# Attention's scores on four quarters of the array, and a unit's outputs in the burst of the next unit's state products

## The chip, the cores and the metric

The kernel runs on one core of a Trainium2 chip. The metric is device time in microseconds (us) of one execution; before the change the median of 3 runs is 1006.01 us (1004.19 to 1006.75).

## The reference, cut to what matters

The first part is a gated linear recurrence over 768 time steps for 4 batches and 8 heads of width 48; its output, as 3072 tokens of width 384, goes through two feed-forward layers.

```python
for t in range(S):
    state = f[:, :, t, :, None] * state + np.einsum('bhd,bhe->bhde', k[:, :, t], v[:, :, t])
    y[:, :, t] = np.einsum('bhd,bhde->bhe', q[:, :, t], state)
...
h = x @ w_in                      # 384 -> 2048, a piecewise square as activation, then 2048 -> 384
...
return (silu * val @ w_out)       # gate and value 384 -> 1536, product, then 1536 -> 384
```

## The kernel before, in words

**Feed-forward passes.** The 3072 tokens are cut into 6 groups of 512. The first layer and the second each take a group in one pass, so there are 12 passes, in the order of `PASSES` (line 34): two groups in layer 1, the same two in layer 2, and so on. A float32 product is made of three matmuls of 128x128 weights with 512 columns (`mm3`, lines 374 to 377: high by high, high by low, low by high), and nine of these (three pieces of 384) are a chunk of the planner: `lin` (578) writes `hp`, `gps` or `vps`, `o_mm` (616) adds to `acc`. During the first pass of each layer the weights, which arrive as 64-bit numbers, are turned into these halves by VectorE, ScalarE and GpSimd (`c_b` to `c_l`, 329 to 360); later passes load them again from DRAM.

**Attention units.** The recurrence is done in 24 units of 128 time steps of one batch (`NU`, line 22), four to a group of tokens. A unit holds its 8 heads as 4 pairs, and its time as two halves of 64 (`C`), so there are 8 blocks. Its steps are:

- `at_k`, `at_q` (460, 465): scaled keys and queries, with rows 0 to 47 for one head of a pair and rows 64 to 111 for the other;
- `at_pe1a` (476): the scores, 16 products of 64x64 over 48 rows. Rows 64 to 111 write partitions 0 to 63 of `psa`, rows 0 to 47 write partitions 64 to 127. All eight blocks lie in one PSUM bank. Each float32 product is two matmul instructions in the trace, so a unit has 32;
- `at_pe1t` (484): four transposes of the keys into `pst`, which ScalarE copies to `kn` (`at_kn`, 503);
- `at_msk` (493): VectorE multiplies the scores by the causal triangle, in two instructions of 64x512, into `ma` and `mb`;
- `at_pe2` (509): the state products of both time halves into `psu0` and `psu1`, 16 products that use rows 0 to 63 and 64 to 127, and both halves of the columns;
- `at_state` (519) on VectorE and `at_state_out` (530) on ScalarE: the new state after each half, copied into `vs`;
- `at_pe3` (535): the outputs `psy` from masked scores and state, 16 products over 112 or 128 rows; `at_yc` (546) copies them to `y`, and for every second unit `at_yd` (556) moves `y` by six DMAs into `xl`, the input of the layer-1 pass; `split_h` and `split_l` (379, 382) make the high and low half of it.

**What sets the order.** Nothing is scheduled at run time. `Planner` (line 49) takes operations with an engine, an estimated duration, dependencies, a priority and buffer slots to take and give. For each engine it takes the ready operation with the smallest priority and writes its instructions, so the engines' queues are fixed, in order, when the kernel is built. Lines 683 to 748 add the attention's operations with priorities around `at_base(u)` (677); the feed-forward's follow in lines 788 to 863. PSUM has eight banks: `at` 3, `h` 2, `acc0` to `acc2`. Before the change `psa`, `pst`, the two `psu` and `psy` all take slots of `at`: `pa` one, `pt` one, `p2` two, `p3` one. Ahead of the first pass TensorE is filled with dummy matmuls (`fill`, 642, tile `wt`).

Of the kernel before, what the change touches and what calls it, by code (L numbers as in the profile page):

```python
# [19 lines left out]
C = 64  # L20
# [28 lines left out]
class Planner:  # L49
# [6 lines left out]
    def add(self, eng, dur, fn, deps=(), prio=0.0, take=(), give=(), lat=None, order=()):  # L56

        lat = lat if lat is not None else {"PE": 0.3, "Pool": 0.25}.get(eng, 0.15)
        deps, order = (tuple(d for d in x if d is not None) for x in (deps, order))
        self.ops.append(dict(eng=eng, dur=dur, fn=fn, deps=deps, order=order, prio=prio, take=take, give=give, lat=lat))  # L60
        return len(self.ops) - 1
# [202 lines left out]
def fast_path(ctx: ExitStack, tc: tile.TileContext, qk, xx, vv, w1, w2, fi, out):  # L264
# [208 lines left out]
        a = A[u]  # L473
        nc.scalar.copy(a["mb"][0:64], a["ma"][0:64])

    def at_pe1a(u):
        a = A[u]
        psa = ps.tile([128, 8, C], F32, tag="at", name="psa", bufs=3)
        for i in range(8):
            nc.tensor.matmul(psa[0:64, i], a["k"][64:112, i], a["ma"][64:112, i], start=True, stop=True)  # L480
            nc.tensor.matmul(psa[64:128, i], a["k"][0:48, i], a["ma"][0:48, i], start=True, stop=True)
        a["psa"] = psa

    def at_pe1t(u):
        a = A[u]
        pst = ps.tile([128, NP, 112], F32, tag="at", name="pst", bufs=3)
        for p in range(NP):
            nc.tensor.transpose(
                pst[:, p], a["t"][:, COLS + p * TB:COLS + (p + 1) * TB], ident[0:112, 0:112]
            )  # L490
        a["pst"] = pst

    def at_msk(u):
        a = A[u]
        tb = tri.rearrange("p (o t) -> p o t", o=1)
        nc.vector.tensor_tensor(
            out=a["ma"][0:64], in0=a["psa"][0:64], in1=tb[0:64].to_broadcast([64, 8, C]), op=ALU.mult
        )
        nc.vector.tensor_tensor(
            out=a["mb"][64:128], in0=a["psa"][64:128], in1=tb[64:128].to_broadcast([64, 8, C]), op=ALU.mult  # L500
        )

    def at_kn(u):
        a = A[u]
        kn = ap_.tile([128, NP, 112], F32, tag="kn", name="kn", bufs=1)
        nc.scalar.copy(kn, a["pst"])
        a["kn"] = kn

    def at_pe2(u):
        a = A[u]  # L510
        a["psu"] = [ps.tile([112, NP, D], F32, tag="at", name=f"psu{c}", bufs=3) for c in range(2)]
        for p in range(NP):
            for c in range(2):
                r = slice(c * C, (c + 1) * C)
                psu = a["psu"][c]
                nc.tensor.matmul(psu[0:64, p], a["kn"][r, p, 0:64], a["vn"][r, 2 * p + 1], start=True, stop=True)
                nc.tensor.matmul(psu[64:112, p], a["kn"][r, p, 64:112], a["vn"][r, 2 * p], start=True, stop=True)
# [17 lines left out]
    def at_pe3(u):  # L535
        a = A[u]
        vs = VS[u % 2]
        psy = ps.tile([112, 8, C], F32, tag="at", name="psy", bufs=3)
        for p in range(NP):
            for c in range(2):  # L540
                i = 2 * p + c
                nc.tensor.matmul(psy[0:48, i], vs[0:112, 0, c, p], a["ma"][0:112, i], start=True, stop=True)
                nc.tensor.matmul(psy[64:112, i], vs[:, 1, c, p], a["mb"][:, i], start=True, stop=True)
        a["psy"] = psy
# [25 lines left out]
    def getX(n):  # L570
        if n not in X:
            X[n] = (xp.tile([128, KK, 512], F32R, tag="xh", name="xh"), xp.tile([128, KK, 512], F32R, tag="xl", name="xl"))
        return X[n]
# [103 lines left out]
    def at_base(u):  # L677
# [2 lines left out]
            return -40.0 + 7.0 * (u % 4)  # L680
        return begin[n - 1] + 4.0 + 15.0 * (u % 4)

    for u in range(NU):
        b = at_base(u)
        n = first1[u // 4]
        if u % 2 == 0:
            E["lx", u] = add("SP", 1.6, lambda u=u: at_loadx(u), (), b - 12, ("x",), (), 2.0, (E.get(("l", u - 1)),))
        E["l", u] = add("SP", 2.1, lambda u=u: at_load(u), (), b - 11.9, ("w" if u < 4 else "qk", "vn"), (), 2.0, (E["lx", u // 2 * 2], E.get(("l", u - 1))))
        E["lv", u] = add("SP", 1.1, lambda u=u: at_loadv(u), (E.get(("p3", u - 2)),), b - 4, (), (), 2.0, (E["l", u],))
        b0 = u // 2 * 2  # L690
        swap = u // 2 in (1, 3)
        if u == b0:
            F = {}

            def mk(u, i, F=F, swap=swap):
                F[i] = decay_ops(u, swap, i)
                F[i][0]()

            if u == 0:
                exs = [  # L700
                    add("ACT", 1.9 - 1.28 * i, lambda i=i, mk=mk: mk(0, i), (E["lx", 0],), b - 3 + i, () if i else ("e",)) for i in range(2)
                ]
                sgs = [add("ACT", 1.9 - 1.28 * i, lambda i=i, F=F: F[i][1](), exs, b - 3 + i) for i in range(2)]
                ads = [add("DVE", 0.45, lambda i=i, F=F: F[i][2](), (exs[i],), b - 2 + i) for i in range(2)]
                for i in range(2):
                    E["sg", i], E["ad", i] = sgs[i], ads[i]
            else:
                ex = add("ACT", 1.07 if u < 8 else 2.35, lambda u=u, mk=mk: mk(u, None), (E["lx", u],), b - 3, ("e",))
                sg = add("ACT", 2.35, lambda F=F: F[None][1](), (ex,), b - 3)
                if swap:  # L710
                    ex, sg = sg, ex
                ad = add("DVE", 0.75, lambda F=F: F[None][2](), (ex,), b - 2)
                for i in range(2):
                    E["sg", u + i], E["ad", u + i] = sg, ad
        odd = u != b0
        one, two = ("x", "e") if swap else ("e", "x")
        R = add("DVE", 1.5, lambda u=u: at_scan_r(u), (E["ad", u],), b)
        Pp = add("DVE", 1.28, lambda u=u: at_scan_p(u), (E["sg", u],), b + 0.2)
        pk = u in POOL_K
        k = add("Pool" if pk else "DVE", 1.8 if pk else 0.7, lambda u=u: at_k(u), (R, E["l", u], E.get(("k", u - 1))), b + 0.1, (), (one,) if odd else ())  # L720
        q = add("DVE", 0.72, lambda u=u: at_q(u), (Pp, E["l", u]), b + 0.4, ("ma", "mb"))
        E["k", u] = k
        so0 = None if u < B else add("ACT", 0.72, lambda u=u: at_state_out(u, 0), (E.get(("st", u - B)), E.get(("p3", u - 2))), b + 1)
        qc = add("ACT", 0.62, lambda u=u: at_qc(u), (q,), b + 1.5)
        pa = add("PE", 1.05, lambda u=u: at_pe1a(u), (k, q), b + 1, ("at",))
        pt = add("PE", 0.35, lambda u=u: at_pe1t(u), (pa,), b + 1.1, ("at",), ("w" if u < 4 else "qk",))
        kn = add("ACT", 0.55, lambda u=u: at_kn(u), (pt,), b + 2, ("kn",), ("at",))
        mask = add("DVE", 1.4, lambda u=u: at_msk(u), (pa, qc), b + 2.5, (), ("at",))
        p2 = add("PE", 0.8, lambda u=u: at_pe2(u), (kn, E["l", u]), b + 3, ("at", "at"), ("kn", "vn"))
        s0 = add("DVE", 0.37 if u < B else 0.75, lambda u=u: at_state(u, 0), (p2, so0, E.get(("st", u - B))), b + 2.2, (), ("at",))  # L730
        so1 = add("ACT", 0.72, lambda u=u: at_state_out(u, 1), (s0, E.get(("p3", u - 2))), b + 2.2)
        s1 = add("DVE", 0.75, lambda u=u: at_state(u, 1), (so1, E.get(("st", u - 1)) if odd else None), b + 4, (), ("at", two) if odd else ("at",))
        E["st", u] = s1
        p3 = add("PE", 1.1, lambda u=u: at_pe3(u), (mask, qc, so1, E["lv", u], E.get(("yc", u - 1))), b + 4, ("at",), ("ma", "mb"))
        E["p3", u] = p3
        E["yc", u] = add("ACT", 1.18, lambda u=u: at_yc(u), (p3,), b + 4, () if odd else ("y",), ("at",))
        if odd:

            tk = ("X",) if u % 4 == 1 else ()
            yd = add(  # L740
                "SP", 3.5, lambda u=u, n=n: at_yd(u, getX(n), u % 4 - 1), (E["yc", u], E["yc", u - 1]), b + 4, tk, ("y",), 2.2,
                (("tx", n),),
            )
            if tk:
                takeX[n] = yd
            sl = slice((u % 4 - 1) * TB, (u % 4 + 1) * TB)
            sh = add("ACT", 0.85, lambda n=n, sl=sl: split_h(*getX(n), sl), (yd,), b + 5)
            E.setdefault(("x", n), []).append(add("DVE", 1.05, lambda n=n, sl=sl: split_l(*getX(n), sl), (sh,), b + 5))
    E["fin"] = add("DVE", 0.6, finish, [E["st", u] for u in range(NU)], 1e6)


# [199 lines left out]
```

## Time and profile before

| | before |
|---|---|
| median of 3 runs | 1006.01 us |
| profiled execution | 1004.98 us |
| span of its trace | 1002.9 us |
| TensorE busy | 966.2 us, 6596 matmuls |
| VectorE busy | 577.5 us |
| ScalarE busy | 490.0 us |
| mean granted TensorE clock | 0.992 |

The span is the time from the first to the last instruction in the trace; the other 2.1 us of the profiled execution lie around it. A matmul's end is modelled in the trace, so two that follow each other overlap in it: the distance from start to start is what one costs. "Busy" adds up what is covered, whether or not it holds anything up.

### The profile page before, as it was taken

What the parts mean: (1) busy time and instruction counts of PE and PEld (TensorE: products, weight loads), DVE (VectorE), ACT (ScalarE), POOL (GpSimd) and SP (SyncE); (2) the same over time, 40 slices, a digit from 0 to 9 for tenths busy, and PEclk for the clock granted to TensorE, in tenths of its full rate; (3) what the DMA queues carried; (4) which work ended last, traced back from release to release, by engine and by line L of the source; (5) the groups of instructions that cost most, each with busy time, mean ns of one, the idle gap of its engine ahead of it and who ended that gap; (6) DMA issues with size and microseconds to landing.
All of it is one profiled execution on the core that took longest, in us unless ns stands there. A gap on an engine that the chain in (4) does not pass through costs nothing.

```text
span 1002.9 us, 16173 instructions
## 1 busy us (share of the span) xinstructions
PE 966.2 (96%) x6596; PEld 790.6 (79%) x6596; DVE 577.5 (58%) x792; ACT 490.0 (49%) x772; POOL 117.6 (12%) x78
## 2 busy tenths in 40 slices
PE   8978797999999999999999999999999999999997
PEld 8956575877878888788888888887877888888885
DVE  6899988986774566575633433474653333433332
ACT  6666576774543446576643212355564544212121
POOL 3344433442320000000000000000000000000000
PEclk9999898999999999999999999999999999999999
DMA  9677766657765676322755102677310554200001
GB/s 276 198 276 255 216 221 235 186 176 267 235 226 176 211 230 196 123 59 70 232 199 170 55 1 67 208 243 227 116 35 17 170 201 165 95 1 12 20 1 35
DMA packets 51954, 153.00 MB, mean 153 GB/s; under 512 B 5744, under 2 KB 25712, under 8 KB 51872
## 3 DMA queue, kind: packets, MB, share of 16 engines
q1 hardware_dynamic: 51872, 151.89, 47.0%
q8 instruction: 54, 0.88, 0.4%
q14 instruction: 28, 0.23, 0.1%
HBM read 110.97 MB, written 36.18 MB: 147 GB/s over the span
## 4 chain that ended last, share of the span: by engine, by line
PE 74%; DVE 10%; DMA 6%; issue 4%; ACT 3%; POOL 2%; SPq 0%; DVEq 0%; ACTq 0%; POOLq 0%
PE acc L375 9%; PE acc L376 9%; PE acc L377 9%; PE hp L375 5%; PE hp L376 5%; PE hp L377 5%; PE vps L375 4%; PE gps L375 4%; DMA raw<-w 4%; PE vps L376 4%; PE gps L376 4%; PE gps L377 4%; PE vps L377 4%; DVE raw L340 2%; PE psa L480 2%
## 5 line engine op out<-in xcount | busy, mean ns | idle before, releaser
L376 PE MATMUL acc<-gl,w 128*128 128x512 f32 x504 | 197.9, 393 | 2.5 <-POOL gl L613 1.8
L375 PE MATMUL acc<-gh,w 128*128 128x512 f32 x504 | 200.1, 397 | 0.0
L377 PE MATMUL acc<-gh,w 128*128 128x512 f32 x504 | 196.9, 391 | 0.0
L375 PE MATMUL hp<-xh,w 128*128 128x512 f32 x288 | 115.7, 402 | 11.4 <-DVE g L596 7.5
L604 DVE TENSOR_TENSOR sg<-gps,sg 128x512 f32<-128x512 f32 x72 | 49.7, 690 | 127.8 <-ACT sg L600 127.8
L376 PE MATMUL hp<-xl,w 128*128 128x512 f32 x288 | 113.4, 394 | 4.3 <-DVE xl L383 4.3
L376 PEld LDWEIGHTS acc<-gl,w 128*128 128x128 f32 x504 | 95.2, 189 | 23.6 <-POOL gl L613 3.3
L377 PE MATMUL hp<-xh,w 128*128 128x512 f32 x288 | 113.0, 392 | 0.0
L375 PEld LDWEIGHTS acc<-gh,w 128*128 128x128 f32 x504 | 95.2, 189 | 21.0 <-ACT gh L608 0.2
L596 DVE SCALAR_TENSOR_TENSOR g<-g,hp 128x512 f32<-128x512 f32 x96 | 65.6, 684 | 79.5 <-ACT g L593 79.3
L377 PEld LDWEIGHTS acc<-gh,w 128*128 128x128 f32 x504 | 95.2, 189 | 19.9
L600 ACT ACTIVATE sg<-gps 128x512 f32<-128x512 f32 x72 | 43.0, 598 | 133.3 <-PE gps L377 122.9
L589 ACT ACTIVATE g<-hp,half 128x512 f32<-128x512 f32 x96 | 66.0, 688 | 75.0 <-PE hp L377 70.5
L608 ACT CAST gh<-sg 128x512 fp32r<-128x512 f32 x72 | 44.7, 620 | 105.3 <-DVE sg L604 105.2
L375 PE MATMUL gps<-xh,w 128*128 128x512 f32 x216 | 85.1, 394 | 0.0
L356 POOL TENSOR_TENSOR w<-raw,w 128x768 fp32r<-128x768 f32 x34 | 70.3, 2066 | 124.6 <-ACT w L352 124.6
L375 PE MATMUL vps<-xh,w 128*128 128x512 f32 x216 | 84.7, 392 | 0.0
L377 PE MATMUL gps<-xh,w 128*128 128x512 f32 x216 | 84.1, 389 | 0.0
L376 PE MATMUL gps<-xl,w 128*128 128x512 f32 x216 | 84.1, 389 | 0.0
L376 PE MATMUL vps<-xl,w 128*128 128x512 f32 x216 | 84.1, 389 | 0.0
L377 PE MATMUL vps<-xh,w 128*128 128x512 f32 x216 | 84.1, 389 | 0.0
L608 ACT CAST gh<-g 128x512 fp32r<-128x512 f32 x96 | 59.5, 619 | 50.3 <-DVE g L596 46.0
(95 smaller groups left out, 1585.1 us busy)
## 6 DMA issues: line engine op xcount, KB each, us to landing
w<-w2d SPq DMA_DIRECT2D x36, 768.0 KB, 4.3
raw<-w SPq DMA_DIRECT2D x34, 768.0 KB, 6.6
w<-w1d SPq DMA_DIRECT2D x32, 768.0 KB, 4.9
w2d<-w SPq DMA_DIRECT2D x18, 768.0 KB, 8.2
w1d<-w SPq DMA_DIRECT2D x16, 768.0 KB, 7.3
qk<-qk SPq DMA_DIRECT2D x24, 448.0 KB, 5.5
x<-xx SPq DMA_DIRECT2D x11, 455.0 KB, 4.4
vn<-vv SPq DMA_DIRECT2D x24, 192.0 KB, 4.8
```

The costliest lines, as they stand in the source:

```text
L340: nc.vector.scalar_tensor_tensor(out=lo, in0=hi, scalar=3, in1=lo, op0=ALU.logical_shift_left, op1=ALU.bitwise_or)
L356: nc.gpsimd.tensor_tensor(out=w[:, :, 1, :], in0=jb["t"].rearrange("p (a n) -> p a n", a=2), in1=w[:, :, 0, :].bitcast(F32), op=ALU.subtract,)
L375: nc.tensor.matmul(o, w[:, 0, wsl], xh, start=first, stop=False)
L376: nc.tensor.matmul(o, w[:, 0, wsl], xl, start=False, stop=False)
L377: nc.tensor.matmul(o, w[:, 1, wsl], xh, start=False, stop=last)
L480: nc.tensor.matmul(psa[0:64, i], a["k"][64:112, i], a["ma"][64:112, i], start=True, stop=True)
L589: nc.scalar.activation(g, hp, AF.Relu, bias=half, scale=0.5)
L596: nc.vector.scalar_tensor_tensor(out=g, in0=g, scalar=1.0, in1=hp, op0=ALU.min, op1=ALU.max)
L600: nc.scalar.activation(sg, gps, AF.Sigmoid)
L604: nc.vector.tensor_tensor(out=sg, in0=p, in1=sg, op=ALU.mult)
L608: nc.scalar.copy(gh, g)
```

## The change

It has three parts.

- The scores of a unit go into two tiles, `psa0` and `psa1`, of four blocks each, in two PSUM banks. In `psa0` the rows and partitions are as before; in `psa1` rows 64 to 111 write partitions 64 to 127 and rows 0 to 47 write partitions 0 to 63. The products are written in an order that goes round these four. The mask is four VectorE instructions of 64x256.
- Scores and transposes are one operation of the planner (`at_pe1`). From unit 4 on it takes all three `at` slots at once; in the first four units its tiles lie in the banks of `acc1`, `acc2` and `h`, without slots of the planner.
- For u of 5 and more that is not the first of its group of four, the outputs of unit u-1 (`at_pe3`) are written right behind the state products of unit u (`at_pe2`) in one operation, which depends on what both need and takes three `at` slots. The last unit of each group, and units 0 to 3, keep an operation of their own for the outputs.

```diff
-    def at_pe1a(u):
...
-        psa = ps.tile([128, 8, C], F32, tag="at", name="psa", bufs=3)
-        for i in range(8):
-            nc.tensor.matmul(psa[0:64, i], a["k"][64:112, i], a["ma"][64:112, i], start=True, stop=True)
-            nc.tensor.matmul(psa[64:128, i], a["k"][0:48, i], a["ma"][0:48, i], start=True, stop=True)
+    def at_pe1(u):
+        tags, bufs = (("acc1", "acc2", "h"), (1, 1, 2)) if u < 4 else (("at",) * 3, (3, 3, 3))
...
+        psa = [ps.tile([128, 4, C], F32, tag=tags[e], name=f"psa{e}", bufs=bufs[e]) for e in range(2)]
+        for i in range(4):
+            for e in range(2):
+                n = i // 2 * 4 + e * 2 + i % 2
+                hi, lo = (slice(64, 128), slice(0, 64)) if e else (slice(0, 64), slice(64, 128))
+                nc.tensor.matmul(psa[e][hi, i], a["k"][64:112, n], a["ma"][64:112, n], start=True, stop=True)
+                nc.tensor.matmul(psa[e][lo, i], a["k"][0:48, n], a["ma"][0:48, n], start=True, stop=True)
...
+    def at_scores(u):
...
+            pv = a["psa"][e].rearrange("p (a c) t -> p a c t", c=2)
+            yield ma[0:64, :, e], pv[hi], hi
+            yield mb[64:128, :, e], pv[lo], lo
...
     def at_msk(u):
...
+        for to, of, r in at_scores(u):
+            nc.vector.tensor_tensor(out=to, in0=of, in1=tb[r].to_broadcast([64, 2, 2, C]), op=ALU.mult)
...
-        pa = add("PE", 1.05, lambda u=u: at_pe1a(u), (k, q), b + 1, ("at",))
-        pt = add("PE", 0.35, lambda u=u: at_pe1t(u), (pa,), b + 1.1, ("at",), ("w" if u < 4 else "qk",))
-        kn = add("ACT", 0.55, lambda u=u: at_kn(u), (pt,), b + 2, ("kn",), ("at",))
-        mask = add("DVE", 1.4, lambda u=u: at_msk(u), (pa, qc), b + 2.5, (), ("at",))
-        p2 = add("PE", 0.8, lambda u=u: at_pe2(u), (kn, E["l", u]), b + 3, ("at", "at"), ("kn", "vn"))
+        pa = pt = add("PE", 1.2, lambda u=u: at_pe1(u), (k, q), b + 1, ("at",) * 3 if u >= 4 else (), ("w" if u < 4 else "qk",))
+        kn = add("ACT", 0.55, lambda u=u: at_kn(u), (pt,), b + 2, ("kn",), ("at",) if u >= 4 else ())
+        mask = add("DVE", 1.7, lambda u=u: at_msk(u), (pa, qc), b + 2.5, (), ("at",) * 2 if u >= 4 else ())
+        fuse = u >= 5 and u % 4 > 0
+        pre = todo.pop() if fuse else None
+        p2 = add(
+            "PE", 1.9 if fuse else 0.8, lambda u=u, fuse=fuse: (at_pe2(u), at_pe3(u - 1) if fuse else None),
+            (kn, E["l", u]) + (pre["deps"] if fuse else ()), b + 3, ("at",) * (3 if fuse else 2),
+            ("kn", "vn") + (("ma", "mb") if fuse else ()),
+        )
+        if fuse:
+            leave(u - 1, p2)
...
-        p3 = add("PE", 1.1, lambda u=u: at_pe3(u), (mask, qc, so1, E["lv", u], E.get(("yc", u - 1))), b + 4, ("at",), ("ma", "mb"))
...
+        deps = (mask, qc, so1, E["lv", u])
+        if u < 4 or u % 4 == 3:
+            deps += (E.get(("yc", u - 1)),)
+            leave(u, add("PE", 1.1, lambda u=u: at_pe3(u), deps, b + 4, ("at",), ("ma", "mb")))
+        else:
+            todo.append(dict(deps=deps + (E.get(("yc", u - 1)),)))
```

`leave(u, p3)` holds, unchanged, what stood behind `p3` in the loop: the copy to `y`, the DMAs into `xl` and the two halves.

## Rows read from the trace of the kernel before

**Rows 1.** The page: span, busy time by engine, and the chain by engine.

```profile
span 1002.9 us, 16173 instructions
...
PE 966.2 (96%) x6596; PEld 790.6 (79%) x6596; DVE 577.5 (58%) x792; ACT 490.0 (49%) x772; POOL 117.6 (12%) x78
...
PE 74%; DVE 10%; DMA 6%; issue 4%; ACT 3%; POOL 2%; SPq 0%; DVEq 0%; ACTq 0%; POOLq 0%
```

**Rows 2.** Stretches: length, then busy us of PE, PEld, DVE, ACT, POOL; PEclk, DMA, GB/s.

```profile
0.00:52.00 52.00, 46.89 (x905) 44.42 (x905) 41.21 (x54) 34.22 (x51) 18.17 (x28) 1.00 0.81 239
52.00:151.00 99.00, 82.10 (x687) 64.10 (x687) 92.12 (x103) 65.55 (x106) 44.62 (x24) 0.97 0.72 242
151.00:300.00 149.00, 141.81 (x630) 114.81 (x631) 117.55 (x137) 88.84 (x125) 54.77 (x28) 0.98 0.68 219
300.00:780.00 480.00, 479.37 (x3424) 388.97 (x3424) 247.99 (x389) 233.64 (x385) 0.00 (x0) 1.00 0.43 138
...
151.00:161.00 10.00, 6.22 (x15) 4.64 (x16) 8.85 (x11) 5.91 (x8) 2.73 (x2) 0.67 0.86 302
```

**Rows 3.** Timeline of TensorE, scores of units 9 and 23: start, us, line, tile.

```profile
332.04 0.39 PE L377 MATMUL acc<-gh,w 128*128 128x512 f32 x1
332.36 0.27 PE L480 MATMUL psa<-ma,qk 48*64 48x64 f32 x1
332.37 0.27 PE L481 MATMUL psa<-ma,qk 48*64 48x64 f32 x1
...
333.29 0.22 PE L481 MATMUL psa<-ma,qk 48*64 48x64 f32 x1
333.44 0.60 PE L488 MATMUL pst<-ident,qk 112*128 112x112 f32 x4
...
334.12 0.39 PE L376 MATMUL gps<-xl,w 128*128 128x512 f32 x1
...
763.09 0.27 PE L480 MATMUL psa<-ma,qk 48*64 48x64 f32 x1
```

**Rows 4.** Timeline of TensorE: the state products of unit 8.

```profile
317.71 0.39 PE L377 MATMUL acc<-gh,w 128*128 128x512 f32 x1
318.03 0.25 PE L516 MATMUL psu<-vn,kn 64*64 64x48 f32 x1
...
318.42 0.29 PE L516 MATMUL psu<-vn,kn 64*64 64x48 f32 x4
...
318.98 0.39 PE L376 MATMUL gps<-xl,w 128*128 128x512 f32 x1
```

**Rows 5.** Groups of VectorE: busy us, mean ns of one, idle before.

```profile
L499 DVE TENSOR_TENSOR mb<-psa,tri 64x512 f32<-64x512 f32 x24 | 16.7, 694 | 0.3
...
L526 DVE TENSOR_TENSOR st<-psu,st 112x192 f32<-112x192 f32 x44 | 15.6, 354 | 20.0 <-PE psu L517 16.7 <-ACT vs L533 2.9
```

**Rows 6.** Timelines of VectorE and TensorE: mask, then state products, of unit 15.

```profile
457.09 0.69 DVE L499 TENSOR_TENSOR mb<-psa,tri 64x512 f32<-64x512 f32 x1
...
458.61 0.25 PE L516 MATMUL psu<-vn,kn 64*64 64x48 f32 x1
```

**Rows 7.** Timelines of TensorE, ScalarE, VectorE: units 4 and 7, and pass 1's start.

```profile
73.05 0.31 PE L542 MATMUL psy<-ma,vs 112*48 112x64 f32 x2 [1.86 <-ACT vs L532]
...
133.89 0.25 PE L516 MATMUL psu<-vn,kn 64*64 64x48 f32 x1
...
137.33 0.35 ACT L533 COPY vs<-st 48x192 f32<-48x192 f32 x1
...
140.97 0.69 DVE L499 TENSOR_TENSOR mb<-psa,tri 64x512 f32<-64x512 f32 x1
...
155.28 0.79 PE L376 MATMUL hp<-xl,w 128*128 128x512 f32 x1 [3.19 <-DVE xl L383]
```

**Rows 8.** Timelines of VectorE and TensorE: the input of pass 9 and its first matmul.

```profile
778.96 0.96 DVE L383 TENSOR_TENSOR xl<-xl,xh 128x768 fp32r<-128x768 f32 x1 [2.15 <-ACT xh L380]
...
781.39 0.39 PE L375 MATMUL hp<-xh,w 128*128 128x512 f32 x1
```

More of the change, by code (lines that the diff above doesn't have):

```diff
@@ L474, in at_qc @@
         nc.scalar.copy(a["mb"][0:64], a["ma"][0:64])
-    def at_pe1a(u):
+    def at_pe1(u):
+        tags, bufs = (("acc1", "acc2", "h"), (1, 1, 2)) if u < 4 else (("at",) * 3, (3, 3, 3))
         a = A[u]
-        psa = ps.tile([128, 8, C], F32, tag="at", name="psa", bufs=3)
-        for i in range(8):
-            nc.tensor.matmul(psa[0:64, i], a["k"][64:112, i], a["ma"][64:112, i], start=True, stop=True)
-            nc.tensor.matmul(psa[64:128, i], a["k"][0:48, i], a["ma"][0:48, i], start=True, stop=True)
+        psa = [ps.tile([128, 4, C], F32, tag=tags[e], name=f"psa{e}", bufs=bufs[e]) for e in range(2)]
[5 more added lines that the diff above has]
+                nc.tensor.matmul(psa[e][lo, i], a["k"][0:48, n], a["ma"][0:48, n], start=True, stop=True)
         a["psa"] = psa
-    def at_pe1t(u):
-        a = A[u]
-        pst = ps.tile([128, NP, 112], F32, tag="at", name="pst", bufs=3)
+        pst = ps.tile([128, NP, 112], F32, tag=tags[2], name="pst", bufs=bufs[2])
         for p in range(NP):
@@ L491, in at_pe1t @@
         a["pst"] = pst
-    def at_msk(u):
[L494 to L501, printed above, removed]
+    def at_scores(u):
+        a = A[u]
+        ma, mb = (a[n].rearrange("p (a e c) t -> p a e c t", e=2, c=2) for n in ("ma", "mb"))
+        for e in range(2):
+            hi, lo = (slice(64, 128), slice(0, 64)) if e else (slice(0, 64), slice(64, 128))
+            pv = a["psa"][e].rearrange("p (a c) t -> p a c t", c=2)
+            yield ma[0:64, :, e], pv[hi], hi
+            yield mb[64:128, :, e], pv[lo], lo
+    def at_msk(u):
+        tb = tri.rearrange("p (a c t) -> p a c t", a=1, c=1)
+        for to, of, r in at_scores(u):
+            nc.vector.tensor_tensor(out=to, in0=of, in1=tb[r].to_broadcast([64, 2, 2, C]), op=ALU.mult)
     def at_kn(u):
@@ L681, in at_base, with leave @@
         return begin[n - 1] + 4.0 + 15.0 * (u % 4)
+    todo = []
+    def leave(u, p3):
+        n, b, odd = first1[u // 4], at_base(u), u % 2
+        E["p3", u] = p3
+        E["yc", u] = add("ACT", 1.18, lambda u=u: at_yc(u), (p3,), b + 4, () if odd else ("y",), ("at",))
+        if odd:
+            tk = ("X",) if u % 4 == 1 else ()
+            yd = add(
+                "SP", 3.5, lambda u=u, n=n: at_yd(u, getX(n), u % 4 - 1), (E["yc", u], E["yc", u - 1]), b + 4, tk, ("y",), 2.2,
+                (("tx", n),),
+            )
+            if tk:
+                takeX[n] = yd
+            sl = slice((u % 4 - 1) * TB, (u % 4 + 1) * TB)
+            sh = add("ACT", 0.85, lambda n=n, sl=sl: split_h(*getX(n), sl), (yd,), b + 5)
+            E.setdefault(("x", n), []).append(add("DVE", 1.05, lambda n=n, sl=sl: split_l(*getX(n), sl), (sh,), b + 5))
     for u in range(NU):
@@ L724, in fast_path @@
         qc = add("ACT", 0.62, lambda u=u: at_qc(u), (q,), b + 1.5)
-        pa = add("PE", 1.05, lambda u=u: at_pe1a(u), (k, q), b + 1, ("at",))
-        pt = add("PE", 0.35, lambda u=u: at_pe1t(u), (pa,), b + 1.1, ("at",), ("w" if u < 4 else "qk",))
-        kn = add("ACT", 0.55, lambda u=u: at_kn(u), (pt,), b + 2, ("kn",), ("at",))
-        mask = add("DVE", 1.4, lambda u=u: at_msk(u), (pa, qc), b + 2.5, (), ("at",))
-        p2 = add("PE", 0.8, lambda u=u: at_pe2(u), (kn, E["l", u]), b + 3, ("at", "at"), ("kn", "vn"))
+        pa = pt = add("PE", 1.2, lambda u=u: at_pe1(u), (k, q), b + 1, ("at",) * 3 if u >= 4 else (), ("w" if u < 4 else "qk",))
[7 more added lines that the diff above has]
+            ("kn", "vn") + (("ma", "mb") if fuse else ()),
+        )
+        if fuse:
+            leave(u - 1, p2)
         s0 = add("DVE", 0.37 if u < B else 0.75, lambda u=u: at_state(u, 0), (p2, so0, E.get(("st", u - B))), b + 2.2, (), ("at",))
@@ L733, in fast_path @@
         E["st", u] = s1
-        p3 = add("PE", 1.1, lambda u=u: at_pe3(u), (mask, qc, so1, E["lv", u], E.get(("yc", u - 1))), b + 4, ("at",), ("ma", "mb"))
[L735 to L748, printed above, removed]
+        deps = (mask, qc, so1, E["lv", u])
[4 more added lines that the diff above has]
+            todo.append(dict(deps=deps + (E.get(("yc", u - 1)),)))
     E["fin"] = add("DVE", 0.6, finish, [E["st", u] for u in range(NU)], 1e6)
```

## The prediction

> **What bounds the kernel now.** I read the page first. TensorE is busy 96% of the span and 74% of the chain that ended last is its own [rows 1]. That is an average, so the second view is the table of stretches [rows 2]. From 300 to 780 us TensorE is busy for 479.37 of 480 us: there a microsecond taken off its stream is a microsecond off the time. Ahead of that it isn't so. From 52 to 151 us, the first layer-1 pass with units 4 to 7 in it, VectorE is busy 92.12 of 99 us and TensorE only 82.10; up to 52 us (units 0 to 3) both have gaps, and TensorE's figure there includes dummy matmuls. So the 24 units fall into 16 (8 to 23) on the bound engine and 8 (0 to 7) where VectorE, DMAs and the order of the units decide. The third view is the timeline of TensorE around single bursts, the fourth the timelines around the start of the second pass.
>
> **The score burst, part by part.** A chunk's matmuls start about 0.227 us apart. In unit 9's burst the last matmul ahead starts at 332.04 and the second one behind it at 334.12, 2.08 us, of which two steps, 0.45 us, would have passed anyway: scores and transposes cost 1.63 us [rows 3]. The 32 score instructions start between 332.36 and 333.29, 0.93 us, in pairs: the two of a pair start 0.01 us apart, and the sixteen pairs about 0.06 us. Of the 16 units on the bound engine 13 have a burst of this shape; the last is unit 23's at 763.09 [rows 3]. The other three have scores and transposes apart, which the change joins; I count nothing for that.
>
> What four quarters give need not be guessed, since the state products use them already. They also are 32 instructions, on both halves of the rows and of the columns, and start between 318.03 and 318.49 (the last row holds four in 0.29 us, of which one takes 0.22) [rows 4]: 0.46 us, about four in the time of two. Their instructions with 64 columns of weights, which the scores have as well, set this end. So I take 0.46 for 0.93, a gain of 0.47 us a unit, and 16 x 0.47 = 7.5 us. The bounds are nothing (two at a time as now) and the same 0.47.
>
> A rule of the Trainium skill speaks against this part. The trace first: today both row halves write one bank, rows 64 to 111 its lower partitions and rows 0 to 47 its upper ones, and the two rows at 332.36 and 332.37 [rows 3] run side by side. The Trainium skill (TensorEngine Tiling (Array Packing), section Restrictions and Gotchas, gotcha 1) says that different row tiles cannot access the same PSUM bank simultaneously. By that rule the new scores, with both row halves in each bank, would not get four at a time; the trace disagrees for disjoint partitions. That four quarters and shared banks go together is shown by no row, so a rival below covers it.
>
> **The joint burst.** The change takes the outputs of 12 of the 16 units (not units 11, 15, 19, 23) from a burst of their own to the end of the next state products. The products stay; one way out of the feed-forward stream and back goes. Into a burst it is 318.03 - 317.71 = 0.32 us and out of it 318.98 - 318.49 = 0.49 us to the second matmul, less two steps: 0.36 us a burst [rows 4]. What joins two kinds of burst is shown by scores and transposes, 333.44 - 333.29 = 0.15 us [rows 3]. I take 0.36 - 0.15 = 0.2 us, 12 x 0.2 = 2.4 us; the bounds are nothing and 0.30 us (a joint like the 0.06 us step), 3.6 us.
>
> So units 8 to 23 give 9.9 us.
>
> **The mask.** An instruction of 64x512 takes 694 ns, one of 112x192 from PSUM 354 [rows 5]; on the line between them 256 columns are 422 ns, and four instead of two cost 1.69 instead of 1.38 us, 0.31 us a unit. The ends are 4 x 354 (nothing more) and 4 x 694 (1.4 us more). From 300 us on VectorE is busy 248 of 480 us [rows 2], so this hides there as long as nobody waits for the mask.
>
> Somebody now can: a joint burst holds the outputs of the unit before, and its two `psu` and one `psy` take all three slots, so **the state products of unit u stand behind the mask of unit u**. They used to wait for the copy `kn` alone. In the TensorE-bound stretch the mask is done first already; the tightest is unit 15, mask until 457.78, products from 458.61 [rows 6], 0.83 us. The new mask is 0.31 us longer and its scores end 0.47 us sooner, so I count nothing. Without that cover TensorE, which is in order, would stand still.
>
> The new input of a pass can be late too. Pass 9's is ready at 779.92 and used at 781.39 [rows 8]: 1.47 us to spare, where a chunk is 9 x 0.227 = 2.05 us. If the last unit slips by a chunk there, up to 0.6 us is lost, and I count nothing.
>
> **The first two stretches.** In pass 0 the mask of unit 7 ends at 141.66, long after the state products at 133.89 [rows 7]: here the new order bites. From these products to the end of the state's copy at 137.68 are 3.8 us; behind a mask at its present place the outputs could start at 141.66 + 3.8 = 145.5 instead of right behind the mask. The outputs of unit 7 lead by copy, six DMAs and the split into halves to the second pass, for which TensorE waits 3.19 us at 155.28 [rows 7]. So 0 us (the planner moves the mask ahead, for which VectorE has to leave weight conversion until later) to 3.8 us; I take half, 1.9. For four more masks on a VectorE that is 93% busy [rows 2] I take 4 x 0.31 = 1.2 us. On the other side unit 4's outputs, which hold TensorE for 1.86 us at 73.05 [rows 7], move to the next unit; half of that, 0.9, I take as gained. Everything else that TensorE saves here (8 x 0.47 + 3 x 0.2 = 4.4 us) I count at nothing, since it waits for others; it is the bound below. Also, the new `psa0` and `psa1` of units 0 to 3 have one buffer each, but a unit's scores come long after the last one's mask. What moves on SP's queue: the `y` DMAs of unit 5 and the `vs` loads that wait for outputs come a unit later. Unit 5's half of the input is ready 40 us ahead of use; I count nothing. Together +2.2 us; the ends are -4.4 - 1.9 = -6.3 and +3.8 + 8 x 0.31 = +6.3 us.
>
> A wait at the pass's start has a tail: from 151 to 161 us the granted clock is 0.67 [rows 2], a mix of the two levels 1.2 and 2.4 GHz, after TensorE had stood still. It is paid before the change too, so I leave it in place.
>
> **Sum.** -7.5 - 2.4 + 2.2 = -7.7 us on the profiled execution of 1004.98 (span 1002.9 and 2.1 around it): 997.3. The median of the runs is 1.0 us above that execution, so 998.3 us.
>
> **Rivals.**
> *No four at a time.* The scores keep their pairs, by the rule above or because tiles share what the state products don't share. Then 7.5 us are missing: 998.3 + 7.5 = 1005.8, no change. Against it speaks [rows 4]; 0.07.
> *Pass 0 shortens as well.* VectorE's order there is free to improve, and TensorE's savings and the wait at 73.05 count in full: 1006.0 - 9.9 - 6.3 = 989.8. With VectorE 93% busy I give 0.06 to anything below 993.
> *TensorE stands at the joint bursts.* The place is the start of each unit's state products. The price is the wait for the mask beyond what is covered; one instruction of another chunk ahead of the mask, such as the 0.69 us of [rows 6], uses up most of the 0.83 us. It decides from (9.9 - 2.2) / 16 = 0.5 us a unit; at 1 us a unit it is 998.3 + 16 = 1014.3, slower. The planner places the products only where it has the mask done, and in 16 units no wait ahead of them shows; 0.08.
> *A late second pass.* The forecast's 2.2 us become 6.3, and the last units of passes 4 and 8 slip too: 1006.0 - 9.9 + 6.3 + 1.2 = 1003.6, no change by the measure below; 0.09.
>
> **How the numbers follow.** The forecast keeps 0.70, between 993.5 and 1002. About 0.3%, 3 us, is what a measurement of this kernel can tell from no change. Faster by more: 0.70 + 0.06 and a part of the late second pass, 0.79. Within: the two cases near 1004 to 1006 give 0.13. Slower: 0.08. The range of 992.5 to 1004 leaves out the standing TensorE, most of the case of pairs and the far end below.
>
> **What would show it.** Right: 32 score instructions within about 0.46 us, bursts of 1.16 us; `psu` and `psy` in one burst of about 1.84 us from unit 5 on; no idle row of TensorE ahead of either from 300 us on; 96 mask instructions of about 420 ns; the stretch of units 8 to 23 about 10 us shorter. Wrong: scores still 0.06 us apart by twos, TensorE waiting for the mask at `psu`, or the second pass starting later than 155 us by more than 4 us.

## The result and the profile after

The changed kernel takes 990.56 us (median of 4 runs, 988.59 to 992.4), the kernel before 1006.38 us beside it: a ratio of 0.9836 [0.9809, 0.9864], 15.8 us less. The ratio and its interval are those on record for the runs; the two medians alone give 0.984. The forecast was 998.3 us with a range from 992.5: the sign is right, the gain twice as large as said, and the time falls below the range. The profiled execution took 991.42 us with a span of 989.4, so 2.0 us lie around it as before.

The page of the changed kernel, the lines of [rows 1]:

```profile
span 989.4 us, 16323 instructions
...
PE 954.5 (96%) x6658; PEld 782.7 (79%) x6658; DVE 583.5 (59%) x840; ACT 490.0 (50%) x772; POOL 114.3 (12%) x78
...
PE 75%; DVE 11%; DMA 6%; issue 3%; ACT 2%; POOL 1%; SPq 1%; DVEq 0%; ACTq 0%; POOLq 0%
```

TensorE is busy 11.7 us less, VectorE 6.0 us more (four mask instructions for two), and TensorE bounds the kernel as before. The stretches, with the columns of [rows 2]; the last line runs from the first matmul of pass 0 to the first of pass 2:

```profile
300.00:780.00 480.00, 479.76 (x3438) 391.46 (x3437) 254.39 (x421) 239.25 (x394) 0.00 (x0) 1.00 0.44 140
151.00:161.00 10.00, 9.44 (x39) 6.66 (x37) 9.49 (x11) 9.03 (x13) 2.82 (x2) 1.00 0.77 262
155.00:165.00 10.00, 7.09 (x29) 4.99 (x28) 9.83 (x13) 9.28 (x15) 3.23 (x2) 1.00 0.90 296
...
55.30:227.80 172.50, 153.57 (x1057) 120.31 (x1058) 162.50 (x189) 122.47 (x187) 77.66 (x42) 0.97 0.75 241
```

The same stretch of the kernel before:

```profile
50.80:230.60 179.80, 155.63 (x1017) 122.76 (x1018) 160.18 (x175) 122.35 (x186) 79.88 (x41) 0.96 0.68 224
```

The two views to compare are these. From 151 to 161 us TensorE was busy 6.22 of 10 us at a granted clock of 0.67 [rows 2]; now it is busy 9.44 at 1.00. Pass 1 starts 4.2 us later in this trace, so the same window does not hold quite the same work: from 155 to 165 us TensorE is busy 7.09 of 10 us, still at 1.00. And passes 0 and 1 together became 179.8 - 172.5 = 7.3 us shorter, 5.2 us of it TensorE's idle time (24.2 to 18.9). So the span's 13.5 us go as follows, by the first matmul of each pass in the two traces:

| stretch | before | after | difference |
|---|---|---|---|
| up to pass 0 | 50.8 | 55.3 | +4.5 |
| passes 0 and 1 (units 4 to 7, start of 8) | 179.8 | 172.5 | -7.3 |
| passes 2 to 10 (rest of unit 8, to 23) | 689.5 | 678.4 | -11.1 |
| pass 11 to the end | 82.8 | 83.2 | +0.4 |

In a second trace of the changed kernel (`after_again`, below) the four differences are +1.7, -5.6, -11.9 and +0.7. The first line is not scatter alone: the five traces with the new bursts in units 0 to 3 start pass 0 between 52.5 and 55.3 us, the nine with the old ones between 49.9 and 52.6. Of the third, 1.2 us is unit 8's transposes and state products (0.41 and 0.81 us), which the plan now puts ahead of pass 2; 9.9 us are left, as forecast (10.7 in the second trace).

TensorE around unit 9's bursts shows why, beside [rows 3] and [rows 4]:

```profile
326.64 0.39 PE L377 MATMUL acc<-gh,w 128*128 128x512 f32 x1
326.95 0.27 PE L486 MATMUL psa<-ma,qk 48*64 48x64 f32 x1
326.96 0.27 PE L487 MATMUL psa<-ma,qk 48*64 48x64 f32 x1
326.97 0.27 PE L486 MATMUL psa<-ma,qk 48*64 48x64 f32 x1
326.98 0.27 PE L487 MATMUL psa<-ma,qk 48*64 48x64 f32 x1
...
327.43 0.22 PE L487 MATMUL psa<-ma,qk 48*64 48x64 f32 x1
327.58 0.60 PE L491 MATMUL pst<-ident,qk 112*128 112x112 f32 x4
...
328.27 0.39 PE L376 MATMUL gps<-xl,w 128*128 128x512 f32 x1
...
329.88 0.39 PE L377 MATMUL gps<-xh,w 128*128 128x512 f32 x1
330.20 0.25 PE L524 MATMUL psu<-vn,kn 64*64 64x48 f32 x1
...
330.81 0.26 PE L550 MATMUL psy<-ma,vs 112*48 112x64 f32 x1
...
331.69 0.22 PE L551 MATMUL psy<-mb,vs 128*48 128x64 f32 x1
...
332.17 0.39 PE L376 MATMUL vps<-xl,w 128*128 128x512 f32 x1
```

Four scores start within 0.03 us, and all 32 in 327.43 - 326.95 = 0.48 us, where it took 0.93. The burst costs 328.27 - 326.64 - 0.45 = 1.18 us for 1.63. State products and outputs follow each other in one burst of 332.17 - 329.88 - 0.45 = 1.84 us, with no idle time ahead of it. The masks, VectorE's groups beside [rows 5]:

```profile
L509 DVE TENSOR_TENSOR mb<-psa,tri 64x256 f32<-64x256 f32 x48 | 20.3, 423 | 0.7
L509 DVE TENSOR_TENSOR ma<-psa,tri 64x256 f32<-64x256 f32 x48 | 20.1, 419 | 4.4 <-PE psa L487 3.5
```

So the late part did what the sum said, and what it did not say lies in passes 0 and 1. There the start of the second pass is what changed. TensorE of the changed kernel, beside the row at 155.28 in [rows 7]:

```profile
155.41 0.39 PE L377 MATMUL acc<-gh,w 128*128 128x512 f32 x1
155.81 0.50 PE L375 MATMUL hp<-xh,w 128*128 128x512 f32 x1
156.82 0.50 PE L376 MATMUL hp<-xl,w 128*128 128x512 f32 x1 [0.50 <-DVE xl L383]
```

Before, it was this, with the row of [rows 7] between the two:

```profile
151.59 0.51 PE L375 MATMUL hp<-xh,w 128*128 128x512 f32 x1 [2.42 <-ACT xh L380]
...
155.87 0.63 PE L377 MATMUL hp<-xh,w 128*128 128x512 f32 x1
156.30 0.63 PE L375 MATMUL hp<-xh,w 128*128 128x512 f32 x1
```

TensorE had waited 2.42 us for the high half of the input, done one matmul, and waited 3.19 us for the low half; the next matmuls then started 0.43 us apart instead of 0.227, the lower of the two clock levels. Now the last sums of pass 0 (`acc`) stand ahead of the new pass's first chunk (`hp`) and last until the input is there. The 5.6 us of waiting are 0.50, and the clock does not fall behind them. A part of the waiting comes back one chunk later, for a gate product (`g`) that VectorE makes behind unit 8's preparation:

```profile
163.35 0.50 PE L375 MATMUL hp<-xh,w 128*128 128x512 f32 x1 [2.38 <-DVE g L604]
```

Nor is the half clock gone from the two passes. Before, the granted clock is 0.50 from 110.0 to 116.8 us and from 154.4 to 161.2; after, from 57.1 to 60.5 and from 135.6 to 142.4, and in the second trace also behind the wait for `g`, from 161.3 to 164.7. Its mean over passes 0 and 1 is 0.96 before, 0.97 and 0.96 in the two traces after. So what the two passes save on balance is mostly waiting.

VectorE changed its order there too. Before:

```profile
149.17 0.70 DVE L441 TENSOR_SCALAR e<-e 112x1040 f32<-112x1040 f32 x1
149.90 2.77 DVE L447 TENSOR_TENSOR_SCAN e<-e,dr 112x520 f32<-112x520 f32 x1
152.71 1.05 DVE L450 SCALAR_TENSOR_TENSOR flag<-e,flag 112x8 f32<-112x8 f32 x1
153.68 0.68 DVE L463 TENSOR_TENSOR qk<-qk,e 112x512 f32<-112x512 f32 x1
154.28 0.94 DVE L383 TENSOR_TENSOR xl<-xl,xh 128x768 fp32r<-128x768 f32 x1
```

After:

```profile
154.41 0.69 DVE L441 TENSOR_SCALAR e<-e 112x1040 f32<-112x1040 f32 x1
155.21 0.69 DVE L634 COPY o<-acc 128x512 f32<-128x512 f32 x1
155.81 0.95 DVE L383 TENSOR_TENSOR xl<-xl,xh 128x768 fp32r<-128x768 f32 x1
156.68 1.23 DVE L447 TENSOR_TENSOR_SCAN e<-e,dr 112x520 f32<-112x520 f32 x1
```

Before, the preparation of unit 8's decay (L441 to L463) took 5.2 us ahead of the input's low half, although the high half was there at 151.53; now the low half goes ahead of the scan. The high half itself is no earlier: it is ready 100.7 us behind pass 0's first matmul before and 100.5 after. Counted from that matmul the split `xl` starts at 154.28 - 50.8 = 103.5 us before and at 155.81 - 55.3 = 100.5 after. Both orders come from the planner, whose estimates the change moved.

### The profile page after: what moved, and what is told of

It reads as the page before. It is cut to its first block, busy times and chain, and to the rows that moved or that the text cites. A ratio compares the mean times of both kernels' runs of the same rounds, so it can differ in the third digit from the quotient of the medians.

```text
span 989.4 us, 16323 instructions
## 1 busy us (share of the span) xinstructions
PE 954.5 (96%) x6658; PEld 782.7 (79%) x6658; DVE 583.5 (59%) x840; ACT 490.0 (50%) x772; POOL 114.3 (12%) x78
## 4 chain that ended last, share of the span: by engine, by line
PE 75%; DVE 11%; DMA 6%; issue 3%; ACT 2%; POOL 1%; SPq 1%; DVEq 0%; ACTq 0%; POOLq 0%
PE acc L375 9%; PE acc L376 9%; PE acc L377 9%; PE hp L375 5%; PE hp L376 5%; PE gps L375 5%; PE vps L375 5%; PE hp L377 5%; PE gps L376 5%; PE gps L377 5%; PE vps L377 5%; PE vps L376 5%; DMA raw<-w 4%; DVE raw L340 2%; PE psy L550 2%
```

## The experiments

Two theories stood first. One: the bursts themselves are worth more than the sum has (each one dropped also spares slow steps behind it), in all 24 units alike. The other: the late units give the 9.9 us forecast and the rest comes from the first two passes. Every variant computes the same function; none leaves work out. Medians stand beside the kernel before on the same chip (1006.6 us in the first group of runs, 1007.25 in the second, 1006.56 in the third).

**The halves of the change.** `quarters_only` keeps the four quarters and gives every unit's outputs a burst of their own again:

```diff
-        fuse = u >= 5 and u % 4 > 0
+        joins = lambda u: u % 4 > 0 and (False)
+        fuse = joins(u)
...
-        if u < 4 or u % 4 == 3:
+        if not joins(u + 1):
```

> Edit: the scores on four quarters and the four-part mask stay, but every unit's outputs have a burst of their own again, as before the change. Theory 1 (a joint burst is worth more than the 0.20 us I counted, because the chunk behind every burst runs slower, so each burst dropped also saves about 0.17 us): 16 units x 0.47 us are saved from the start of pass 2 to the start of pass 11, about 7 us less than the kernel before, which takes 689.5 us there; the small slow steps behind bursts stay at the kernel before's 6.8 us in passes 3 to 8 (after the change 4.7). Rival (the slow steps belong to the old scores): they fall to about 4.7 us here too, and the stretch is 9 us shorter. In the first two passes: if the joint bursts took TensorE's waits away there, the waits at units 4 to 7 come back and passes 0 and 1 take about 178 us instead of 172.5; if the four quarters or the later start did it, they take 172.5 again.

Measured: 994.93 us, 0.9886 [0.9841, 0.9931].

`joint_only` keeps the joint bursts, with scores, transposes and mask as before:

```diff
-        pa = pt = add("PE", 1.2, lambda u=u: at_pe1(u), ...
+        pa = add("PE", 1.05, lambda u=u: at_pe1a(u), (k, q), b + 1, ("at",))
+        pt = add("PE", 0.35, lambda u=u: at_pe1t(u), (pa,), b + 1.1, ("at",), ("w" if u < 4 else "qk",))
...
+        mask = add("DVE", 1.4, lambda u=u: at_msk_old(u), (pa, qc), b + 2.5, (), ("at",))
```

> Edit: outputs join the next unit's state products as in the change, but scores and mask are the ones of before, in one bank and two instructions. Theory 1: from the start of pass 2 to the start of pass 11 it saves 12 x (0.20 + 0.17) = 4.5 us against the kernel before's 689.5 us. Rival (only the way in and out counts): 2.4 us. Passes 0 and 1: 172 to 174 us if the joint bursts took away the waits of TensorE at units 4 to 7, about 179 as before if not.

Measured: 1001.11 us, 0.9946 [0.9928, 0.9964]. The gains of the halves, 11.7 and 5.5 us, add up to 17.2 for 15.8 together, so neither needs the other. In passes 2 to 10 they are 9.0 and 4.1 us. Of the 9.0, 1.2 us are unit 8's moved steps and 0.7 less waiting (TensorE stands 1.26 us there before, 0.58 here); 7.1 are left, 0.47 for each of the 15 score bursts in these passes (unit 8's is in pass 1). Of the 4.1, 0.4 us are unit 8's transposes, which this plan moves too, and 0.4 less waiting (0.83 us here); 3.3 are left. The steps behind a burst speak against the first theory: behind unit 9's transposes seven steps go from 328.27 to 329.88, 0.230 us each for 0.227, so slow steps are worth some 0.02 us a burst, not 0.17.

Passes 0 and 1 take 174.1 us in `quarters_only` and 177.9 in `joint_only`, so most of what is gained there comes with the quarters' half of the edit. In both plans the last sums stand ahead of pass 1's first chunk, but in `joint_only` TensorE still waits 3.67 us for the low half, at 160.73.

**The units.** `from_unit8` leaves units 0 to 7 as before, `from_unit4` units 0 to 3:

```diff
+        if u >= 8:        # the new operations; from_unit4: u >= 4
...
-        fuse = u >= 5 and u % 4 > 0
+        joins = lambda u: u % 4 > 0 and (u >= 9)        # from_unit4: u >= 5, as in the change
+        fuse = joins(u)
```

> Edit: units 0 to 7 are as before the change, all that is new begins with unit 8. Theory 2 (the late part alone gives 11 us, the first two passes the rest): pass 2 starts at 230.6 us as before, within 2 us, and the time is 1005 - 11 = 994 us, so 0.989 of before. Rival (the late part draws its gain from what happened early): more than 3 us off that.

> Edit: units 0 to 3 are as before the change, all that is new begins with unit 4. The first pass then starts near 50.8 us as before and not at 55.3 us. Theory 3 (the new bursts of units 4 to 7 shorten passes 0 and 1 from 179.8 to 172.5 us whatever the start): pass 2 starts near 223.3 us and the time is some 4 us below the changed kernel's 990.6. Rival (the late start was the reason, since VectorE gets ahead with the weights while TensorE fills; work of VectorE sets when pass 2 starts): pass 2 starts near 227.8 us again and the time is the changed kernel's, within 2 us.

Measured: `from_unit8` 998.07 us, 0.9916 [0.9891, 0.9941]; `from_unit4` 989.36 us, 0.9828 [0.9782, 0.9875], and in five further rounds (`from_unit4_again`) 991.07 us, 0.9848 [0.9827, 0.9869], as the changed kernel itself, run again (`after_again`): 990.75 us, 0.9843 [0.9817, 0.9869].

> The changed kernel once more, for the scatter: the starts of passes 0, 1 and 2 (55.3, 155.8, 227.8 us) within 1.5 us, from pass 2 on within 0.5 us of the same length (678.4 us to pass 11); the time within 988 to 993 us.

> Units 0 to 3 as before the change, the rest as in the changed kernel, once more with more rounds: the first pass starts at 50 to 52 us, pass 2 at 224.3 within 1.5, the time 987 to 990.5 us, 0.980 to 0.984 of before.

So the gain is not alike in all units: units 8 to 23 alone give 8.5 us, about the forecast's 9.9; units 4 to 7 give some 7.6 us more, and units 0 to 3 nothing that can be measured in the time. `from_unit8` still has both waits at the second pass's start, 2.46 and 3.19 us. It is 4.1 us above the 994 us that was expected of it (0.9916 of the kernel before for 0.989), more than the 3 us at which the expectation turns to its rival, and the rival has a share: passes 2 to 10 take 680.2 us there for 678.4 and 677.6, with 2.55 us of standing TensorE for 1.08 and 0.25. `from_unit4` starts pass 2 at 224.3 us (225.4 again) for 227.8 and 226.6, but its time is no lower: its passes 2 to 10 take 679.2 and 680.3 us.

**The order at the start of the second pass.** `after_input_first` is the changed kernel with pass 1's first chunk put back ahead of pass 0's last two chunks of sums; `before_sums_first` is the kernel before with that first chunk behind the last sums:

```diff
+            if n == 1 and j == 0:        # after_input_first
+                for o in P.ops[late:]:
+                    if o["eng"] == "PE" and o["prio"] > bo14 - 0.01 and o is not P.ops[hm]:
+                        o["order"] += (hm,)
...
             back = oms[-lag - 1:][:1] if len(oms) > lag else []
+            if n == 1 and j == 0:        # before_sums_first
+                back = oms[-1:]
```

> Edit, to the changed kernel: one dependency more, so that the first chunk of pass 1 stands ahead of the last two chunks of sums of pass 0 in TensorE's queue, as it did before the change. Attention is as in the changed kernel. Theory 4: the stop comes back, TensorE waits 4 to 7 us for the input of pass 1 and runs on at half the clock for some matmuls; pass 2 starts at 232 to 235 us instead of 227.8 and the time rises by 4 to 7 us. Rival: no change in pass 2's start beyond 1.5 us.

> Edit, to the kernel before the change: one dependency more for the planner, so that the first chunk of pass 1 (which needs unit 7's output) stands behind the last sums of pass 0 in TensorE's queue and not ahead of two of them. Attention is untouched. Theory 4 (the missing part of the gain is the stop at the second pass's start: TensorE in order behind a chunk whose input is late, 2.6 + 3.5 us, and some 13 matmuls at half the clock, 2.8 us): the two chunks of sums run while the input is on its way, the stop shrinks from about 9 to 2 to 4 us, pass 2 starts at 224 to 226 us instead of 230.6, and the time falls by 4 to 6 us. Rival (the change's shorter bursts at units 4 to 7 make the gain there): pass 2 starts at 230.6 us, within 1.5.

Measured: `after_input_first` 997.0 us, 0.9898 [0.9874, 0.9923]: 6.3 us of the 7.6 are gone (against `after_again`, 990.75 us). Its TensorE and the stretch from 151 to 161 us:

```profile
155.61 0.80 PE L375 MATMUL hp<-xh,w 128*128 128x512 f32 x1 [4.64 <-ACT xh L380]
158.36 0.79 PE L376 MATMUL hp<-xl,w 128*128 128x512 f32 x1 [1.96 <-DVE xl L383]
158.96 0.63 PE L377 MATMUL hp<-xh,w 128*128 128x512 f32 x1
159.38 0.63 PE L375 MATMUL hp<-xh,w 128*128 128x512 f32 x1
```

```profile
151.00:161.00 10.00, 3.43 (x7) 2.44 (x8) 9.86 (x12) 7.40 (x11) 2.56 (x2) 0.70 0.78 228
```

The two waits are back, with the half clock behind them. `before_sums_first` took 1007.13 us, 0.9999 [0.998, 1.0019]: nothing, where 4 to 6 us were expected. Its TensorE:

```profile
152.65 0.50 PE L375 MATMUL acc<-gh,w 128*128 128x512 f32 x1 [0.96 <-ACT gh L608]
156.28 0.50 PE L376 MATMUL acc<-gl,w 128*128 128x512 f32 x1 [3.12 <-POOL gl L613]
156.61 0.43 PE L377 MATMUL acc<-gh,w 128*128 128x512 f32 x1
156.84 0.62 PE L375 MATMUL acc<-gh,w 128*128 128x512 f32 x1
```

There the sums stand and wait, for `gl`, which the plan of before gives late, to GpSimd. TensorE's order alone is not enough; what it waits for must be early as well.

**The other queues.** `before_prep_later` is the kernel before with the decay preparation of units 8 and 9 held back until pass 1's ninth chunk; `before_both` adds the sums first; `from_unit4_prep_later` does it to `from_unit4`:

```diff
+        if u == 8: prep = [ex, sg]
+        if u == 10: P.ops[ex]["deps"] += (prep[0],)
...
+            if n == 1 and j == 8:
+                for i in prep: P.ops[i]["deps"] += (hm,)
```

> Edit, to the kernel before the change: the decay preparation of units 8 and 9 (their first two ScalarE steps, and with them the additions and scans on VectorE) waits for the ninth chunk of pass 1. In the kernel before, VectorE does 5.2 us of it from 149.17 to 154.36 us, ahead of the split of pass 1's input (154.28 to 155.22, its other half ready at 151.53) and of the last gate products of pass 0. Attention's bursts are untouched. Theory 5 (it is this place in VectorE's queue, which the change's plan happens to move, that made the stop at the second pass's start): the split runs right behind 151.5, TensorE's stop shrinks from about 9 us to 5 or less, and pass 2 starts at 225 to 228 us instead of 230.6. Rival (the shorter bursts themselves): 230.6 within 1.5.

> Edit, to the kernel before the change: both the preparation of units 8 and 9 later and the last sums of pass 0 ahead of pass 1's first chunk. Attention's bursts are untouched. Theory 5: VectorE and GpSimd have the operands of the last sums ready in time, so these run while the input is on its way; stop of 1 to 3 us, pass 2 starts at 223 to 226 us and the time falls by 5 to 7 us, with no change to attention. Rival: as before within 1.5 us.

> Edit, to the changed kernel: units 0 to 3 as before the change, and the preparation of units 8 and 9 later, as in the run on the kernel before. Theory 5: the wait of 2.5 us for VectorE's gate product in pass 1 (at 159.6 us with units 0 to 3 as before) goes as well; pass 2 starts at 221 to 223 us instead of 224.3, and the time is 2 us less than without this, 985 to 988 us. Rival: the work only moves to another wait in pass 1, no difference.

Measured: 1004.06 us, 0.9971 [0.9956, 0.9986]; 1003.45 us, 0.9971 [0.9956, 0.9987]; 991.69 us, 0.9866 [0.9844, 0.9888]. VectorE of `before_prep_later`:

```profile
151.99 1.40 DVE L613 TENSOR_TENSOR gl<-g,gh 128x512 fp32r<-128x512 f32 x1 [1.06 <-ACT gh L608]
153.32 2.01 DVE L383 TENSOR_TENSOR xl<-xl,xh 128x768 fp32r<-128x768 f32 x1
```

Counted from pass 0's first matmul the split starts at 153.32 - 52.1 = 101.2 us for 103.5, but it takes 2.01 us for 0.94. With both edits passes 0 and 1 last 175.6 us, for 179.8 before and 172.5 and 174.1 after. Pass 2 then starts at 227.5 us, as early as in the changed kernel, which starts pass 0 later. But in `before_both` TensorE still waits 2.58 us for `gl` at 154.39 and runs at half clock behind it. So edits to the order of the old kernel show about 3 us of the gain, where 5 to 7 were expected. In `from_unit4` the same edit gains nothing: the wait of 2.40 us for `g` at 159.60 goes, but passes 0 and 1 take 173.7 us for 173.0 and 174.3, and unit 8's state products move behind the start of pass 2.

**Bank by bank.** `paired_order` writes all scores of one bank and then those of the other:

```diff
-        for i in range(4):
-            for e in range(2):
+        for e in range(2):
+            for i in range(4):
```

> Edit, to the changed kernel: the scores of a unit are written first bank by first bank (all of psa0, then all of psa1), so that only two quarters can run at a time; tiles, mask, plan and joint bursts stay. Theory (rate): 32 score instructions take 0.93 us again, units 8 to 23 lose 16 x 0.47 = 7.5 us, all of it from pass 1's psa of unit 8 to the end; what is gained in passes 0 and 1 comes from the plan and stays within 2 us (172 to 175 us). Rival (faster scores make the gain in passes 0 and 1): they take 177 us or more.

Measured: 995.26 us, 0.9895 [0.9862, 0.9928]. The scores of unit 9 start between 325.85 and 326.60, 0.75 us for 0.48, and passes 2 to 10 keep 681.9 us for 678.4 and 677.6. That is not the 0.93 us expected; 16 x 0.27 = 4.3 us fit the 4.5 us by which the run is slower than `after_again`. Passes 0 and 1 still last only 174.4 us. So the order of the four quarters matters where TensorE is the bound, and the early gain does not hang on fast scores.

## Why the prediction was wrong in size

**Four quarters: right.** 0.48 us for the forecast 0.46, burst 1.18 us for 1.16. The Trainium skill (TensorEngine Tiling (Array Packing), Restrictions and Gotchas, gotcha 1) bars different row tiles from one PSUM bank at a time. The trace does not agree for disjoint partitions: both row tiles write each bank, and four start within 0.03 us. By that rule the 7.5 us would be missing. The rival "no four at a time" falls.

**Joint burst: right.** 331.69 - 329.88 and the way out, 1.84 us, as forecast, and the late part as a whole came out at 9.9 us. `joint_only` alone takes some 3.3 us from passes 2 to 10 by way of the joint, against the term's 2.4 and its bound of 3.6, so the term was a little small.

**Mask: right.** 419 and 423 ns for the 422 on the line. Nobody waits for it from 300 us on: TensorE is busy 479.76 of 480 us, and unit 9's last mask instruction ends at 329.43, 0.77 us ahead of its products. The rival of the standing TensorE falls.

**The first two stretches: the step that failed.** The prediction put three terms there, +1.9 + 1.2 - 0.9 = +2.2 us; the runs give about -7.6 (998.07 to some 990.5), 9.8 us apart and past the stated end of -6.3.
- "Everything else that TensorE saves here ... I count at nothing, since it waits for others": wrong. What it waited for moved as well: TensorE's idle time in passes 0 and 1 went from 24.2 to 18.9 us (19.2 in the second trace).
- "It is paid before the change too, so I leave it in place", said of the half clock behind the wait at the second pass's start: wrong. The wait itself, of which [rows 7] show 3.19 us, was priced only as something that could grow. Wait and half clock at this place are the largest part: with both back, `after_input_first` loses 6.3 us.
- Unit 7's chain, +1.9 between 0 and 3.8: it came out at the lower end, nothing. The planner moved unit 7's mask ahead of the state products, and its outputs are copied 148.00 - 55.3 = 92.7 us after the pass's first matmul (93.7 in the second trace), before 144.56 - 50.8 = 93.8.
- Unit 4's stall of 1.86 us at 73.05 is gone from its place; its share was not measured alone.

The rival that named it was "Pass 0 shortens as well" at 989.8 us, with 0.06: its condition, that VectorE's order is free to improve, is part of what happened. That its time is right within 1 us is in part luck: its sum counts TensorE's savings and unit 4's stall and has no term for the second pass's start. It was held down by VectorE's 93%, a mean over a stretch, though 5.2 us of VectorE's work at the decisive place was for a unit not yet needed.

**What stays open.** That the order on TensorE's queue carries 6.3 us in the changed kernel is shown by undoing it (the waits it brings back, with the half clock, are in that figure); that it is worth nothing by itself in the old one is shown too. How the gain of units 4 to 7 divides between TensorE's order, VectorE's order, unit 4's stall and TensorE's shorter bursts was not separated further: the edits to the order of the old kernel show about 3 us. That the new bursts of units 0 to 3 start pass 0 some 3 us later and do not show in the time is seen in the traces, and why is open too. Why the planner chose the new order (its estimate puts unit 7's outputs behind a later burst, so the sums come first) is argued from its rules, not tested.

## What to carry to other kernels

Price a change of a planned kernel in two sums: what the bound engine saves where it is the bound, and separately what every in-order queue does at the next stage boundary, since a new duration or dependency makes the planner write another order there. A wait that the profile shows at such a boundary, with the half clock behind it, is a term with both signs: here 5.6 us of waiting and a stretch at 0.67 could go as well as grow. Test it by moving one operation back, and look at all queues: in the old kernel TensorE's order alone gained nothing while VectorE and GpSimd kept theirs.

## What was not expected of the hardware

In `paired_order` instructions on a free quarter of the array start ahead of earlier ones whose quarter is busy. There 16 instructions of the first bank stand ahead of those of the second, yet TensorE's timeline has:

```profile
325.85 0.27 PE L486 MATMUL psa<-ma,qk 48*64 48x64 f32 x1
...
326.13 0.22 PE L487 MATMUL psa<-ma,qk 48*64 48x64 f32 x1
326.14 0.27 PE L486 MATMUL psa<-ma,qk 48*64 48x64 f32 x1
326.15 0.27 PE L487 MATMUL psa<-ma,qk 48*64 48x64 f32 x1
326.19 0.22 PE L486 MATMUL psa<-ma,qk 48*64 48x64 f32 x1
...
326.60 0.22 PE L487 MATMUL psa<-ma,qk 48*64 48x64 f32 x1
```

The two of 0.27 us, the duration of each quarter's first in the bursts above, start as the eleventh and twelfth, while six of the first bank are still to come (the trace marks the one that reports the first bank done at 326.31, as the 21st of the 32, where in order it would be the 16th); from 326.24 on four go in each 0.06 us until the first bank is done. So 32 scores take 0.75 us, not the 0.93 of two at a time.
